# Opening of a fused Mamba-2 scan and hard-swish MLP: C loaded by heads, second weights queued behind the row sums, decode steps reordered

## The chip, the cores and the metric

The kernel runs on one core of one Trainium2 chip. The metric is the device time of one execution in microseconds (us), lower is better. Engines are named as in the profile: PE (TensorE), PEld (its weight loads), DVE (VectorE), ACT (ScalarE), POOL (GpSimd), SP (SyncE, which only issues DMAs here). A "q" behind a name is the engine's sequencer.

## The reference

Two blocks follow each other. The first is a chunked state-space scan over x (4, 8, 768, 32), a (4, 8, 768), B and C (4, 8, 768, 16); the second an MLP of width 2048 on the result, seen as 3072 tokens of 256.

```python
log_a = np.log(np.clip(a, 1e-06, 1.0))
for c in range(nc):                                  # chunks of 32 tokens
    cum = np.cumsum(la, axis=-1)
    L = np.exp(cum[:, :, :, None] - cum[:, :, None, :]) * causal
    CB = np.einsum('bhin,bhjn->bhij', Cc, Bc)
    y_intra = np.einsum('bhij,bhjd->bhid', CB * L, xc)
    y_inter = np.einsum('bhin,bhnd->bhid', Cc, state) * np.exp(cum)[..., None]
    y[:, :, sl] = y_intra + y_inter
    state = decay_full * state + np.sum(Bx, axis=2)  # Bx: B x^T, faded to the chunk's end
...
h = x @ w_in                                         # (3072, 256) @ (256, 2048)
g = h * np.clip(h + 3.0, 0.0, 6.0) / 6.0
out = (g @ w_out).astype(np.float32)                 # (3072, 2048) @ (2048, 256)
```

The weights w_in and w_out arrive as 64-bit floats and everything else as 32-bit.

## The kernel before

The kernel takes the sequence in six chunks of 128 tokens (`NC` = 6), all 4 batches (`NB`) and 8 heads (`NH`) at once. Each chunk goes through the scan and then, as 512 tokens, through the MLP; chunk c + 1's scan is woven into chunk c's MLP. The first chunk has no MLP to hide behind, so the program begins with an **opening** that runs chunk 0's scan alone. The order of all instructions is written out by hand; each engine takes its own in that order, and waits where data or a buffer is not there.

**Decay matrices of chunks 0 and 1.** `a` is loaded, its logarithm taken, and the row sums formed in two parts: `add_up(ends_at[0])` for the first 256 tokens, `add_up(ends_at[1])` for the rest (L269). The first part is split in three bf16 pieces (`in_three`), and TensorE builds the differences of the sums in PSUM: `diff_mask` (L336), `mask_again` (L343), `diff_less` (L348), `diff_pick` (L357). ScalarE takes the exponentials (`diff_exp`, L365; `first_eto`, L376). The second part is stored to DRAM by `store_rows` as `cum_e` and `cum_d` (L286, L288) and read back later, broadcast over rows. `turn_cum` and `by_token` turn the sums of chunks 2 to 5 (L316, L319), for use much later.

**Chunk 0's scan.** `turn_b` transposes B on TensorE (L422) and copies it as `bT` (L431). C comes by another way: `pairs_first` loads it already by pairs of heads in eight DMAs (L101), into a tile whose row is 32 times the pair plus a group of four tokens; `turn_squares` (L465) then turns 32x32 blocks on VectorE, and `part_heads` (L475) makes the two masked copies `cT`. `ends` (L396) and `fade` (L481) run on GpSimd. `scores(0)` multiplies them on TensorE (L530), then forms the chunk's contribution to the state from `xt` (L548). `multiply(0)` takes the part sums out on ScalarE (L564, L574) and applies the decay on VectorE (four L579). `mix(0)` (L625, and L503 for the state) gives y, `keep(0)` copies it out (four L639), `renew(0)` makes the next state (L600, two L558). `busy(n, bank)` issues n matmuls whose result nobody reads (L493). After that `mlp_in` begins (L647): 16 values of f, two matmuls each, in four PSUM banks, with `ramp` (L754, ScalarE) and `times_ramp` (L759, VectorE) behind each; then `first_out` (L772).

**Weights.** w_in and w_out come in four quarters each, i = 0 to 7 (`NP` = 4: i < 4 is w_in, f = 4i to 4i + 3), as raw 64-bit words through three buffers. `load_w(i)` issues the DMA of a quarter (L139), and `decode(i)` turns it into 32-bit floats by bit operations on two engines. A decode is a generator; `weights(i, n)` runs n of its five steps: (1) ACT takes the top words (L198), and with quarter 0 DVE the significand (L201, L205); (2) DVE L215, L217 (and L201 with other quarters); (3) ACT L221 (and L205); (4) ACT L223, and the load of quarter i + 3 when i > 0; (5) DVE L228 and L236, which writes the decoded weights. Quarters 0 and 1 are decoded in the opening, the later ones between the values of f.

**DMA order.** Quarter 0 and B of chunk 0 are issued by ACT, everything else by SP in this order: `a`, eight of C, x, quarter 1, `cum_e`, `cum_d`, quarters 2, 3 and 4, then chunk 1's loads. A DMA's completion is counted in one of eight semaphores; a DMA that reuses a semaphore waits for the one before it there, so the sixth C load waits for quarter 0, the seventh for `a`, the eighth for the first C load. Chunks 2 to 5 load B and C by `pairs_first` too.

Of the kernel before, what the change touches and what calls it, by code (L numbers as in the profile page):

```python
# [8 lines left out]
FP32 = mybir.dt.float32  # L9
# [5 lines left out]
ALU = mybir.AluOpType  # L15
# [6 lines left out]
def kernel(  # L22
# [24 lines left out]
    nc = tc.nc  # L47
    P = 128
    NB, NH, S, D = x.shape
# [18 lines left out]
    ps = ctx.enter_context(tc.tile_pool(name="ps", bufs=1, space=PSUM))  # L68
# [17 lines left out]
    def load_bc(c):  # L86

        sl = slice(c * P, (c + 1) * P)  # L90

        def tokens_first(src, queue=nc.sync, **where):
            t = loads.tile([P, NB * NH, N], FP32, **where)
            queue.dma_start(out=t, in_=src[:, :, sl, :].rearrange("b h s n -> s (b h) n"))
            return t

        def pairs_first(src):
            t = loads.tile([P, 2, NB, 4, N], FP32, name="pairs", tag="bc")
            for b in range(NB):
                for h in range(2):  # L100
                    nc.sync.dma_start(  # L101
                        out=t[:, h, b].rearrange("s a n -> s (a n)"),
                        in_=src[b, h:NH:2, sl, :].rearrange("h (s a) n -> h s (a n)", a=4))
            return t

        if 0 < c < TURN:
            bcs[c] = [tokens_first(C, name="C", tag="bc")]
        Bs[c] = tokens_first(B, nc.scalar if c == 0 else nc.sync, name="B", bufs=1)
        if c == 0:
            bcs[c] = [pairs_first(C), Bs[c]]  # L110
        elif c < TURN:
            bcs[c].append(Bs[c])
        else:
            bcs[c] = [pairs_first(C), pairs_first(B)]

    def load_x(c):
        sl = slice(c * P, (c + 1) * P)
        xts[c] = loads.tile([P, NB * NH, D], FP32, name="xt", bufs=1)
        nc.sync.dma_start(out=xts[c], in_=x[:, :, sl, :].rearrange("b h s d -> s (b h) d"))
# [8 lines left out]
    def load_w(i, queue=nc.sync):  # L128

        raw = loads.tile([P, NK * FP * 2 * P], U32, name="raw", bufs=NRAW)  # L130
        if i < NP:
            cols = slice(2 * i * FP * P, 2 * (i + 1) * FP * P)
            src = moe_w_in[:, cols].rearrange("(k p) f -> p k f", p=P)
            dst = raw.rearrange("p (k f) -> p k f", k=NK)
        else:
            r0 = (i - NP) * FP * P
            src = moe_w_out[r0:r0 + FP * P, :].rearrange("(k p) m -> p k m", p=P)
            dst = raw.rearrange("p (k m) -> p k m", k=FP)
        queue.dma_start(out=dst, in_=src)  # L139
        raws[i] = raw  # L140
# [1 line left out]
    load_w(0, nc.scalar)  # L142
    load_bc(0)
    load_x(0)
    load_w(1)
    nc.scalar.preload_act_table_set("natural_log_exp_and_others")


# [6 lines left out]
    def conceal_in(t, pattern):  # L155
# [24 lines left out]
        out=head, in_=head, pattern=[[-2 * N, NQ], [-N, 2]], compare_op=ALU.is_ge,  # L180
        fill=0.0, base=0, channel_multiplier=1)
    nc.gpsimd.affine_select(
        out=head, in_=head, pattern=[[2 * N, NQ], [N, 2]], compare_op=ALU.is_ge,
# [3 lines left out]
    def decode(i):  # L187

        n = NK * FP * P
        top = raws[i].bitcast(U16).rearrange("p (n w) -> p n w", w=4)[:, :, 3]
        lo, hi = (raws[i].rearrange("p (n w) -> p n w", w=2)[:, :, w] for w in range(2))
        s = att.tile([P, n], U16, name="ws")
        e = att.tile([P, n], U16, name="we")
        m = att.tile([P, n], U32, name="wm")
        nc.scalar.copy(out=s, in_=top)  # L198

        def significand():  # L200
            nc.vector.tensor_scalar(  # L201
                out=m, in0=hi, scalar1=0xFFFFF, scalar2=0x100000,
                op0=ALU.bitwise_and, op1=ALU.bitwise_or)
            yield
            nc.vector.scalar_tensor_tensor(  # L205
                out=m.bitcast(FP32), in0=lo, scalar=2.0 ** -32, in1=m, op0=ALU.mult,
                op1=ALU.add)
            yield

        parts_m = significand()  # L210
        if i == 0:
            next(parts_m)
            next(parts_m)
        yield
        nc.vector.tensor_scalar(  # L215
            out=e, in0=s, scalar1=0x7FF0, scalar2=None, op0=ALU.bitwise_and)
        nc.vector.tensor_scalar(  # L217
            out=s, in0=s, scalar1=0x8000, scalar2=None, op0=ALU.bitwise_and)
        next(parts_m, None)
        yield  # L220
        nc.scalar.activation(e.bitcast(BF16), e, AF.Relu, bias=bias_hi, scale=-8.0)  # L221
        yield
        nc.scalar.activation(e, e.bitcast(BF16), AF.Relu, bias=bias_lo, scale=-1.0)  # L223
        next(parts_m, None)
        if i and i + NRAW < 2 * NP:
            load_w(i + NRAW)
        yield
        nc.vector.tensor_tensor(out=e, in0=e, in1=s, op=ALU.bitwise_or)  # L228
        m, e = m.bitcast(FP32), e.bitcast(BF16)
        if i < NP:  # L230
            dst = w_in[i]
            m, e = (t.rearrange("p (k f) -> p k f", k=NK) for t in (m, e))
        else:
            dst = w_out[:, (i - NP) * FP:(i - NP + 1) * FP, :]
            m, e = (t.rearrange("p (k f) -> p k f", k=FP) for t in (m, e))
        nc.vector.scalar_tensor_tensor(  # L236
            out=dst, in0=m, scalar=2.0 ** -20, in1=e, op0=ALU.mult, op1=ALU.mult)
# [47 lines left out]
    def store_rows():  # L285
        nc.sync.dma_start(  # L286
            out=cum_e[1:].rearrange("c g p -> g c p"), in_=cum_c[:, 1:])
        nc.sync.dma_start(  # L288
            out=cum_d[2:].rearrange("c a g i -> g (c a) i"),
            in_=cum[:, 2 * P:].rearrange("g (k i) -> g k i", i=HT))  # L290
# [21 lines left out]
    cum_n = const.tile([P, NC, G], FP32, name="cum_n")  # L312
# [3 lines left out]
            nc.tensor.transpose(out=c_ps[:, c], in_=cum_c[:, c], identity=ident[:G, :G])  # L316

    def by_token(c_ps):
        nc.vector.tensor_scalar(  # L319
            out=cum_n[:, 2:], in0=c_ps[:, 2:], scalar1=-1.0, scalar2=None, op0=ALU.mult)  # L320


    yTs, states, mids, bTs, bss, tmps = {}, {}, {}, {}, {}, {}
# [17 lines left out]
    def mask_again(c, b):  # L341

        nc.tensor.matmul(  # L343
            out=ds[c, b], lhsT=ident_h, rhs=hide.unsqueeze(1).to_broadcast([P, NH, HT]),
            start=True, stop=True)
# [45 lines left out]
    def ends(c, b):  # L391

        if b == 0:
            bss[c] = att.tile([P, G, N], FP32, name="bs", bufs=1)
        hs = slice(b * NH, b * NH + NH)
        nc.gpsimd.tensor_tensor(  # L396
            out=bss[c][:, hs], in0=Bs[c][:, hs],
            in1=Ls[c][:, b, :, HT - 1:HT].to_broadcast([P, NH, N]), op=ALU.mult)
# [8 lines left out]
    def turned(c):  # L407
        if c not in bTs:
            bTs[c] = [att.tile([P, NB, P], FP32, name="bT", bufs=1),
                      att.tile([P, NB, 2, P], FP32, name="cT", bufs=1),  # L410
                      att.tile([P, NB, P], FP32, name="csT", bufs=1)]
        return bTs[c]

    def turn_ps(c, j):

        if c < 2:
            return ps.tile([P, NB, P], FP32, name="t_ps", tag=f"f{2 * j if c else 1}")
        return ps_o.tile([P, NB, P], FP32, name="t_ps", tag="o")

    def transposes(c, j, t_ps):  # L420
        for b in range(NB):
            nc.tensor.transpose(  # L422
                out=t_ps[:, b],
                in_=bcs[c][j][:, b * NH:(b + 1) * NH].rearrange("s h n -> s (h n)"),
                identity=ident)

    def turn_b(c):

        t_ps = turn_ps(c, 1)
        transposes(c, 1, t_ps)  # L430
        nc.scalar.copy(out=turned(c)[0], in_=t_ps)  # L431
# [58 lines left out]
    def busy(n, bank):  # L490

        for _ in range(n):
            nc.tensor.matmul(  # L493
                out=bank.rearrange("p (b i) -> p b i", b=NB), lhsT=ident,
                rhs=ident.unsqueeze(1).to_broadcast([P, NB, P]), start=True, stop=True)
# [514 lines left out]
    def weights(i, n):  # L1010
        for _ in range(n):
            next(parts[i], None)
# [12 lines left out]
    row_signs()  # L1025
    add_up(ends_at[0])
    in_three()
    for b in range(3):
        mask_again(0, b)
    diff(0, 0, 1)  # L1030
    diff(0, 2, 3)
# [5 lines left out]
    weights(0, 1)  # L1037
    for b in range(NB):
        ends(0, b)
    turn_b(0)  # L1040
    diff(1, 0, 1)
    weights(0, 1)
    diff_exp(1, 2)
    diff_exp(1, 3)
    turn_squares(bcs[0][0], turned(0)[2])
# [1 line left out]
    fade(0, HALF[1], nc.gpsimd)  # L1047
    add_up(ends_at[1])
    store_rows()
    load_w(2)  # L1050
    weights(0, 1)
    busy(2, ps.tile([P, NB * P], FP32, name="d", tag="f3"))
    scores(0)
    multiply(0)
    load_w(3)
    c_ps = ps.tile([P, NC, G], FP32, name="c_ps", tag="f1")
    turn_cum(c_ps)
    busy(1, ps.tile([P, NB * P], FP32, name="d", tag="f0"))
    weights(0, 1)
    weights(1, 1)  # L1060
    by_token(c_ps)
    mix(0)
    keep(0)
    weights(1, 3)
    renew(0)
    weights(1, 1)
    load_eto(1)
    load_bc(1)
    load_x(1)
# [175 lines left out]
```

## Time and profile before

| What | us |
|---|---|
| time, median of 3 runs (339.91 to 340.11) | 339.91 |
| profiled execution, its own time | 339.78 |
| its span in the trace | 337.6 |
| PE busy | 330.6 (98%) |
| DVE busy | 234.5 (69%) |
| ACT busy | 199.4 (59%) |
| POOL busy | 123.9 (37%) |
| first `mlp_in` matmul (L647) begins, in the chain of waits | 22.60 |
| first `first_out` matmul (L772) begins, in the chain of waits | 50.27 |

Times in the trace count from the span's start. A row of the timeline has start, length, engine, line, operation, output and inputs, a count, and in brackets the idle time before it and what ended that. The chain of waits goes back from the last instruction to whatever released each step. DMA rows stand at the time of issue and their length is the issue, not the transfer.

### The profile page before, as it was taken

How to read it: one execution, taken by the hardware profiler on the slowest of the kernel's cores; microseconds unless marked ns; L12 is line 12 of the kernel's file. 1: busy time of each engine (PE TensorE's matmuls, PEld its weight loads, DVE VectorE, ACT ScalarE, POOL GpSimd, SP SyncE). 2: the span in 40 equal slices, each digit the busy share in tenths (PEclk: the TensorE clock that was granted, in tenths of full speed). 3: DMA queues.
4: the chain of work that ended last, by engine and by line, in shares of the span. 5: the costliest groups of instructions: out<-in, count | busy, mean ns of one | idle time of the engine just before them, and what ended most of it. 6: DMA issues, size and time to landing. Idle time of an engine off the chain costs nothing.

```text
span 337.6 us, 8192 instructions
## 1 busy us (share of the span) xinstructions
PE 330.6 (98%) x3337; PEld 265.4 (79%) x3337; DVE 234.5 (69%) x380; ACT 199.4 (59%) x418; POOL 123.9 (37%) x123
## 2 busy tenths in 40 slices
PE   6999999999999999999999999999999999999996
PEld 2554448888888888888888888888888888899995
DVE  6699999998399739755339556355477355599974
ACT  4769878757986670576461576570486030577661
POOL 3300000290184799089813079911079800000000
PEclk9999999999999999999999999999999999999999
DMA  8999968042590215258107267101160001110001
GB/s 174 165 316 201 208 219 184 2 54 76 139 142 1 57 37 139 33 72 78 33 13 156 33 83 69 28 4 17 27 81 2 2 2 18 26 21 2 1 2 62
DMA packets 89605, 25.15 MB, mean 75 GB/s; under 512 B 82208, under 2 KB 85952, under 8 KB 89056
## 3 DMA queue, kind: packets, MB, share of 16 engines
q1 hardware_dynamic: 85184, 23.33, 37.5%
q10 hardware_dynamic: 4384, 1.31, 1.8%
q8 instruction: 26, 0.43, 0.5%
q14 instruction: 11, 0.09, 0.1%
HBM read 21.33 MB, written 3.29 MB: 73 GB/s over the span
## 4 chain that ended last, share of the span: by engine, by line
PE 94%; DMA 3%; DVE 1%; SPq 1%; issue 0%; DVEq 0%
PE h L715 33%; PE wb L914 13%; PE wc L914 8%; PE o L772 8%; PE h L647 8%; PE wa L914 8%; PE o_end L880 6%; PE y L625 3%; PE y L503 2%; PE cb L530 2%; DMA raw<-in_moe_w_in_dram 2%; DMA pairs<-in_C_dram 1%; PE y L548 1%; SPq L101 1%; PE o_end L898 1%; PE sp L548 0%
## 5 line engine op out<-in xcount | busy, mean ns | idle before, releaser
L759 DVE SCALAR_TENSOR_TENSOR gT<-gT,h 128x512 f32<-128x512 f32 x96 | 64.8, 684 | 33.8 <-ACT gT L754 32.2
L754 ACT ACTIVATE gT<-h,half 128x512 f32<-128x512 f32 x96 | 65.2, 685 | 25.6 <-PE h L715 23.6
L735 ACT ACTIVATE h<-h 128x512 f32<-128x512 f32 x66 | 38.2, 585 | 39.0 <-PE h L715 38.8
L715 PE MATMUL h<-y_hi,w_part 128*128 128x512 f32 x160 | 51.5, 407 | 0.0
L715 PE MATMUL h<-y_less,w_part 128*128 128x512 f32 x160 | 50.1, 399 | 0.0
L715 PE MATMUL h<-y_lo,w_part 128*128 128x512 f32 x160 | 49.5, 395 | 0.0
L818 POOL TENSOR_TENSOR s<-gT 128x512 f32<-128x512 f32 x16 | 23.8, 1490 | 46.7 <-DVE gT L759 46.7
L715 PEld LDWEIGHTS h<-y_lo,w_part 128*128 128x128 f32 x160 | 30.0, 188 | 7.3
L715 PEld LDWEIGHTS h<-y_hi,w_part 128*128 128x128 f32 x160 | 30.0, 188 | 6.8 <-DVE gT L759 0.2
L715 PEld LDWEIGHTS h<-y_less,w_part 128*128 128x128 f32 x160 | 29.2, 188 | 6.0 <-ACT h L735 0.2
L385 ACT ACTIVATE L<-L,cum_n 128x64 f32<-128x64 f32 x128 | 31.6, 336 | 0.0
L772 PE MATMUL o<-w_out,gT 128*128 128x256 f32 x128 | 28.8, 381 | 0.0
L647 PE MATMUL h<-yT,w_in 128*128 128x512 f32 x64 | 27.7, 594 | 0.0
L772 PEld LDWEIGHTS o<-w_out,gT 128*128 128x128 f32 x128 | 24.1, 190 | 3.8 <-issue 0.5
L647 PEld LDWEIGHTS h<-yT,w_in 128*128 128x128 f32 x64 | 12.1, 190 | 14.9 <-issue 13.2
L158 POOL TENSOR_SCALAR_AFFINE_SELECT L<-L 64x1024 f32<-64x1024 f32 (+1 forms) x16 | 20.4, 1281 | 8.5 <-DMA L<-cum_d 8.0
L579 DVE TENSOR_TENSOR L<-L,cb 128x512 f32<-128x512 f32 x24 | 15.0, 681 | 11.7 <-PE cb L530 11.7
L403 POOL TENSOR_TENSOR tmp<-state,eto 128x256 f32<-128x256 f32 x5 | 3.2, 643 | 52.8 <-ACT eto L389 48.9
L818 POOL TENSOR_TENSOR s<-gT,s 128x512 f32<-128x512 f32 x16 | 21.7, 1364 | 0.9
L396 POOL TENSOR_TENSOR bs<-B,L 128x128 f32<-128x128 f32 x24 | 11.2, 486 | 29.5 <-ACT L L385 20.9
L880 PE MATMUL o_end<-v_pair,g_pair 128*128 128x256 f32 x120 | 21.1, 281 | 0.0
L818 POOL TENSOR_TENSOR gT<-gT 128x512 f32<-128x512 f32 x16 | 20.4, 1279 | 0.9
(140 smaller groups left out, 593.0 us busy)
## 6 DMA issues: line engine op xcount, KB each, us to landing
raw<-in_moe_w_out_dram SPq DMA_DIRECT2D x4, 1024.0 KB
L<-cum_d SPq DMA_DIRECT2D x8, 512.0 KB
xt<-in_x_dram SPq DMA_DIRECT2D x6, 512.0 KB
raw<-in_moe_w_in_dram SPq DMA_DIRECT2D x3, 1024.0 KB
out_dram<-back SPq DMA_DIRECT2D x128, 16.0 KB
pairs<-in_C_dram SPq DMA_DIRECT2D x40, 32.0 KB
eto<-cum_e SPq DMA_DIRECT2D x20, 64.0 KB
B<-in_B_dram SPq DMA_DIRECT2D x5, 256.0 KB
```

Source lines behind the costliest of these rows:

```text
L158: nc.gpsimd.affine_select(out=t[rows], in_=t[rows], pattern=pattern, compare_op=ALU.is_ge, fill=-1e5, base=base, channel_multiplier=-1)
L385: nc.scalar.activation(Ls[c][:, b, h], Ls[c][:, b, h], AF.Exp, bias=cum_n[:, c, g:g + 1])
L579: nc.vector.tensor_tensor(out=Ls[c][:, :, hs], in0=Ls[c][:, :, hs], in1=cbs[c][q], op=ALU.mult)
L647: nc.tensor.matmul(out=h, lhsT=w_in[f // FP][:, j, f % FP * P:(f % FP + 1) * P], rhs=yTs[k][:, j].rearrange("p b i -> p (b i)"), start=(j ...
L715: nc.tensor.matmul(out=hs_[k, f], lhsT=w[j][:, f % FP * P:(f % FP + 1) * P], rhs=y[:, j], start=(start and j == 0), stop=True, skip_group_ ...
L735: nc.scalar.activation(h, h, AF.Copy, scale=1.0 / EPS + 1.0)
L754: nc.scalar.activation(gTs[k][:, f], h, AF.Relu, bias=half, scale=1.0 / 6.0)
L759: nc.vector.scalar_tensor_tensor(out=g, in0=g, scalar=1.0, in1=h, op0=ALU.min, op1=ALU.mult)
L772: nc.tensor.matmul(out=o[:, b % 2], lhsT=gTs[0][:, f, b * P:(b + 1) * P], rhs=w_out[:, f], start=(f == 0 and b % 2 == 0), stop=True, skip_ ...
L818: nc.gpsimd.tensor_tensor(out=o, in0=p_, in1=q_, op=op)
L880: nc.tensor.matmul(out=ends_["cross" if n == 2 else "squares"][b], lhsT=g_parts[t][n][:, b * P:(b + 1) * P], rhs=w, start=(t == 0 and b < ...
L914: nc.tensor.matmul(out=bank[:, slot], lhsT=lhs[:, j], rhs=rhs[:, j], start=(clear and j == 0), stop=True, skip_group_check=True)
```

## The change

Line numbers here and below are those of the kernel before. Six things change:

1. `pairs_first` still makes eight DMAs, but one for each head with all batches, instead of one for each batch and half of the heads. The destination of one is 32 rows by 4 batches by 64 elements, the source the same, with the 32 groups of four tokens outermost; before, it was 128 rows by 64 elements, with four heads outermost in the source. The pieces have 64 elements in both.
2. `load_w(1)` moves from behind `load_x(0)` to behind `store_rows()`: on SP it now follows `cum_e` and `cum_d`.
3. In `decode`, quarter 1 runs its significand operations (L201, L205) in steps 1 and 2 instead of 2 and 3; quarter 0 and the later ones are unchanged.
4. `by_token` is a ScalarE multiplication instead of a VectorE one, and stands ahead of quarter 0's last step, the mix and `keep`.
5. `mask_again` also runs for batch 3; quarter 0's third step (L221) moves ahead of `turn_b(0)`; `busy(2, ...)` ahead of `scores(0)` is gone, `busy(1, ...)` stays.
6. All five steps of quarter 1 follow `renew(0)`; before, L198 stood ahead of `keep`, L215 to L223 ahead of `renew`, the fifth step behind it.

```diff
         def pairs_first(src):
             t = loads.tile([P, 2, NB, 4, N], FP32, name="pairs", tag="bc")
-            for b in range(NB):
-                for h in range(2):
-                    nc.sync.dma_start(
-                        out=t[:, h, b].rearrange("s a n -> s (a n)"),
-                        in_=src[b, h:NH:2, sl, :].rearrange("h (s a) n -> h s (a n)", a=4))
+            for h in range(NH):
+                rows = slice(h // 2 * 32, h // 2 * 32 + 32)
+                nc.sync.dma_start(
+                    out=t[rows, h % 2].rearrange("s b a n -> s b (a n)"),
+                    in_=src[:, h, sl, :].rearrange("b (s a) n -> s b (a n)", a=4))
             return t
...
     load_x(0)
-    load_w(1)
...
         parts_m = significand()
-        if i == 0:
-            next(parts_m)
+        for _ in range(2 - i):
             next(parts_m)
...
     def by_token(c_ps):
-        nc.vector.tensor_scalar(
-            out=cum_n[:, 2:], in0=c_ps[:, 2:], scalar1=-1.0, scalar2=None, op0=ALU.mult)
+        nc.scalar.mul(cum_n[:, 2:], c_ps[:, 2:], -1.0)
...
-    for b in range(3):
+    for b in range(NB):
         mask_again(0, b)
...
     for b in range(NB):
         ends(0, b)
+    weights(0, 1)
     turn_b(0)
     diff(1, 0, 1)
-    weights(0, 1)
...
     store_rows()
+    load_w(1)
     load_w(2)
     weights(0, 1)
-    busy(2, ps.tile([P, NB * P], FP32, name="d", tag="f3"))
     scores(0)
     multiply(0)
     load_w(3)
     c_ps = ps.tile([P, NC, G], FP32, name="c_ps", tag="f1")
     turn_cum(c_ps)
     busy(1, ps.tile([P, NB * P], FP32, name="d", tag="f0"))
+    by_token(c_ps)
     weights(0, 1)
-    weights(1, 1)
-    by_token(c_ps)
     mix(0)
     keep(0)
-    weights(1, 3)
     renew(0)
-    weights(1, 1)
+    weights(1, 5)
     load_eto(1)
```

## The prediction

> **What bounds the kernel now.** I read the page first, its chain of work that ended last.
> ```profile
> PE 94%; DMA 3%; DVE 1%; SPq 1%; issue 0%; DVEq 0%
> ```
> TensorE sets the end almost everywhere; 6% do not belong to it, and the next view, the chain in order of time for the first 60 us, shows that they lie in the opening.
> ```profile
> 0.80 5.94 DMA raw<-in_moe_w_in_dram
> ...
> 8.91 4.00 DMA pairs<-in_C_dram
> ...
> 13.09 1.17 DVE csT L465
> ...
> 14.28 0.89 DVE cT L475 x2
> ...
> 15.30 1.25 PE cb L530 x59
> ...
> 17.90 0.43 PE c_ps L316 x4
> ...
> 22.60 27.66 PE h L647 x64
> 50.27 9.93 PE o L772 x46
> ```
> Columns: start, length, work. Until 13 us the chain is the first weights and then C's eight loads; after that it goes C's turn, scores, mix, and from 22.60 the first linear layer. Third, the timeline by engine, for what is moved.
> ```profile
> 10.65 0.39 ACT L376 ACTIVATE eto<-e_ps 128x256 f32<-128x256 f32 x1
> 11.95 0.59 ACT L431 COPY bT<-t_ps 128x512 f32<-128x512 f32 x1 [0.90 <-PE t_ps L422]
> 18.75 1.15 ACT L198 COPY ws<-raw 128x1024 uint16<-128x1024 uint16 x1 [0.53 <-DMA raw<-in_moe_w_in_dram]
> 22.65 0.37 ACT L639 COPY yT<-y 128x256 f32<-128x256 f32 x1 [0.26 <-PE y L503]
> 22.92 1.15 ACT L221 ACTIVATE we<-we,bias_hi 128x1024 bf16<-128x1024 uint16 x1
> 26.01 1.23 DVE L236 SCALAR_TENSOR_TENSOR w_in<-wm,we 128x1024 f32<-128x1024 f32 x1
> 33.62 1.22 DVE L236 SCALAR_TENSOR_TENSOR w_in<-wm,we 128x1024 f32<-128x1024 f32 x1
> 41.11 1.22 DVE L236 SCALAR_TENSOR_TENSOR w_in<-wm,we 128x1024 f32<-128x1024 f32 x1
> 48.12 1.23 DVE L236 SCALAR_TENSOR_TENSOR w_out<-wm,we 128x1024 f32<-128x1024 f32 x1
> ```
> The first four rows show ScalarE idle for 0.90 us before bT and busy with the decode of the second weights around `keep`. The L236 rows end the decodes of quarters 1 to 4, at 27.24, 34.84, 42.33, 49.35: 7.6, 7.5 and 7.0 us apart, while TensorE takes 27.66/16 x 4 = 6.9 us for the four f that use a quarter. Quarter 4 (w_out's first) is done 0.92 us before its first use at 50.27. The decode is a second bound right behind TensorE.
>
> **C's loads.** In the trace's completion events each C load raises its semaphore by one lump and four single steps; loads that lead with 128 rows (B, xt, raw) or 32 rows (pre, cum_e) do it in sixteen. So a load that leads with 4 heads runs on 4 of the 16 queues, and B agrees: twelve of its parts land by 9.28, four at 10.18 to 11.15. With 32 rows outermost each C load should run on sixteen, with 64 of its 256-byte pieces in each instead of 256 in four. Issue: the sixth load still waits for the first weights (6.74) and starts at 6.76; the seventh took 1.49 us against full queues, now 0.57 like the sixth; the eighth starts at about 8.0 instead of 8.91. C loads of later chunks land 2.5 to 3.1 us after their issue. That gives 10.5; bounds 9.8 (pieces hidden) and 12.9 (as before).
>
> **To the scores.** VectorE has been free since 10.23. L465 starts at 10.5 + 0.18 = 10.7, the two L475 end 2.08 later at 12.8, add_up (L269) 3.19 later at 13.9. ScalarE now does L221 (1.15) ahead of bT: 11.06 to 12.2, mostly in the idle 0.90; bT ends at 12.8 instead of 12.54, a loss only if it comes last; behind it stand two L365 and L223, not wanted before 16 us. TensorE ends chunk 1's differences at 12.96 as now (B's transposes begin at 11.28, and TensorE was not free before 11.17, so an earlier B brings nothing). All three meet: scores at 13.0 instead of 15.30, **2.3 us earlier**. `busy(2)` (1.98) would hold TensorE until 14.9, so its removal is needed for 1.9 of these; alone it would bring nothing, since 0.43 us of idle follows it. The fourth `mask_again` costs 0.43, under TensorE's idle 0.52 before 7.50.
>
> **Scores to the linear layer**, 15.30 to 22.60, keeps its links and its 7.3 us: add_up is done (13.9) before the products L579 start (14.3), and VectorE's second L579 holds c_ps as now. xt is issued at 8.6 instead of 9.59; its four late parts took 2.7 us after C, the others about 4, so it lands at 13.2 to 14.5; L548 wants it at 14.1, and until 14.7 a delay hides behind L579. GpSimd's fade (L481, 1.51) follows L475 and ends at 14.3, wanted only in the mix. `by_token` on ScalarE costs between 0.21 (L257) and 0.39 (L376) where ScalarE waits for the mix, with the copies of `keep` behind it; on VectorE it was 0.28 behind L236, and ended at 21.10, in the mix. I take 0 for it, bounds -0.1 and 0. The layer starts at 20.3.
>
> **The second weights.** Their load leaves its place behind xt (10.43) for one behind cum_e and cum_d, which wait for add_up: cum_e 13.9, and by the old spacing (16.31 to 17.17) the load 0.86 later, 14.8. The first weights took 5.94 from issue to landing, the last quarter 5.6 with the queues empty: 20.4 to 20.7, where it landed at 18.73 before. Queued behind it are quarters 2 and 3, needed at 25 and 31 us; they follow 3 to 4 us apart and are in time. L198 of quarter 1 now stands behind `keep`, whose last copy ends at 23.02 - 2.3 = 20.7. So the load arrives as it is wanted, with nothing to spare: 0, bounds 0 and +2.4 (below).
>
> **Decode of quarter 1.** L198 20.7 to 21.9, L215 21.9 to 22.35, L221 at 22.4, against 22.92. VectorE finishes quarter 0 (L228, L236) at 18.6 and `renew` (L600, 2 x L558: 1.03) at 19.7, takes L201 when the load lands, and waits for L198: `renew` ahead of the decode is free, and the early L201 too (0.7 in a wait). From L221 on the steps are as before, so the chain of decodes moves by **0.55 us** only, and L236 ends at 26.7. VectorE sets its pace: 4 x 0.68 (L759) and 0.42 + 0.43 + 0.69 + 1.22 + 0.69 + 1.22 for a quarter make 7.4, less some overlap.
>
> **Sum.** TensorE would come to w_out at 50.27 - 2.3 = 47.97; quarter 4 is ready at 49.35 - 0.55 = 48.80 and TensorE starts 0.13 later (as 15.17 to 15.30): 48.93. The gain is 50.27 - 48.93 = **1.34**; 0.96 of 2.3 is given back as waits in the first layer. Behind it the next slacks are larger: w_out's second quarter has 1.45 (55.75 for 57.2), chunk 1's L579 ends 1.4 before the mix at 77.98, and the later C and B loads are on no wait of the chain. The profiled execution took 339.78 (span 337.6, 2.2 around it), the median is 0.13 higher: 339.91 - 1.34 = 338.6.
>
> **Rivals.** (a) The second weights come late. From 20.7 on each us costs one, since decodes have no other cover; from 22.0 the gain is gone. One load (issue 39.94) had fifteen parts by 45.54 and one at 47.47, 7.5 after issue; its own row before is 8.3, behind xt. That gives 22.3 to 23.1, 1.6 to 2.4 late: 340.2 to 341.0. For it: a single slow queue appears in three of eight weight loads; against it: the queues are empty at 14.8. This is the way to slower. (b) C's loads land no sooner, at 12.9: scores at 15.3, L198 behind `keep` at 23.0 and L221 at 24.65, 1.73 later than now; less the 0.8 of slack at w_out, +0.9: 340.8. The break-even is a landing at about 12. The Trainium skill (DMA: Bandwidth & Descriptors, "Rules for kernel authors") speaks for it: transfers split over disjoint partitions share the same engines and only serialize. The trace does not bear this out, as the loads before did not use all sixteen. (c) Decode keeps up at its fastest pace, 7.0 a quarter: all 2.3 stay, 337.6. Against it: two of three steps are 7.5. (d) TensorE slows without `busy`. Its first eleven 512-column matmuls come 0.43 apart (8 in 3.57 us), from 7.50 the spacing is about 0.22, after 5.4 us of work. Were that lost before the linear layer, 5.4 us would do the work of 2.7 and w_out be reached at 50.7: +0.4, 340.3. Against it: before, small matmuls fill 14.9 to 22.5 but for one `busy(1)`, which stays, and the layer starts at 0.43 a pass; the longest gap that I expect is 0.5 us. The Trainium skill (TensorE: Matmul & The Clock Gate, "What's actually happening") has the gate close only after some 3.4 us idle; by that rule nothing changes here.
>
> **Chances.** Forecast 0.62, (a) 0.14, (b) 0.06, (c) 0.10, (d) 0.05, others 0.03. Within 0.2% means 0.68 us, about what measuring this kernel can tell from no change. Half of (a) and most of (d) stay within it, and in a few of the forecast's cases the load is 0.7 late. Faster 0.70, same 0.14, slower 0.16. The range goes from (c), 337.6, to the middle of (a), 340.6.
>
> **To be seen after.** Sixteen steps for each C load, L465 at 10.4 to 11, scores at about 13.0, the first L647 at 20.3, quarter 1's L198 at 20.7 behind `keep` and not behind DMA, L236 ends near 26.7, 34.2, 41.8 and 48.8, short waits of L647 on VectorE (about 1 us together), the first L772 at 48.9. Wrong if L465 waits for C beyond 12, if L198 waits for the load, or if L647's first pass takes over 0.43.

## The result: slower, and the profile after

| | median of 13 runs, us | range |
|---|---|---|
| before | 340.23 | 339.64 to 342.23 |
| after | 342.82 | 339.56 to 345.77 |

The ratio is 1.0053, 95% interval 1.003 to 1.0077: the kernel became slower by half a per cent, some 1.8 us. The medians take all runs; the ratios here and below leave out those more than 1.5% above the fastest of their kernel, which are three of after here and five of the twelve of "after, with `busy(2)` back" below, its profiled one among them. The forecast of 338.6 and its range are wrong.

The profiled execution of after is the quickest of its thirteen, 339.56 us with a span of 337.4, and the only one with a granted clock of 1.00 throughout (the share of TensorE's full clock that the profile records); the other twelve show means of 0.984 to 0.998. So the profile shows what the change does when almost nothing disturbs it, and a second question is what happens in the others. Line numbers of after are two or three lower (L644 is the old L647, L219 the old L221, L234 the old L236). The chain of waits by engine:

```profile
PE 85%; DVE 6%; DMA 4%; ACT 3%; issue 1%; SPq 0%
```

TensorE had 94% of it before. The same chain in order of time (start, length, work; in this view a DMA's length runs from its issue to its landing):

```profile
1.73 6.55 DMA pairs<-in_C_dram
...
8.29 7.03 DMA xt<-in_x_dram
...
18.95 0.28 issue
...
21.96 1.04 ACT ws L197
...
23.48 1.16 ACT we L219
...
41.67 1.24 DVE w_in L234
...
42.95 7.13 PE h L644 x16
50.09 12.07 PE o L769 x55
```

x has taken C's place as the last load that TensorE waits for, and from 21.96 the chain runs through the decode of the second weights until w_in's last quarter is written at 42.91. `first_out` begins at 50.09 instead of 50.27: in this run the change is worth 0.18 us up to there. The timeline shows where the forecast 2.3 us went (in brackets the idle time before, and what ended it):

```profile
11.82 1.11 DVE L462 STREAM_TRANSPOSE csT<-pairs 128x512 f32<-128x512 f32 x1 [1.85 <-DMA pairs<-in_C_dram]
14.00 1.20 PE L527 MATMUL cb<-cT,bT 32*64 32x128 f32 x64 [1.44 <-DVE cT L472]
15.46 1.16 PE L545 MATMUL y<-xt,bs 64*32 64x64 f32 x64 [0.27 <-DMA xt<-in_x_dram]
23.48 1.15 ACT L219 ACTIVATE we<-we,bias_hi 128x1024 bf16<-128x1024 uint16 x1 [0.49 <-DVE we L213]
```

C landed at 11.64, not 10.5, so the scores start at 14.00 and not at 13.0, and TensorE, without `busy(2)`, stands idle for 1.44 us. One row of the chain above is new: 0.28 us of "issue" in the middle of the mix, a time in which TensorE waits for nothing that the profile knows. It turned out to be the key.

### The profile page after: what moved, and what is told of

It reads as the page before. It is cut to its first block, busy times and chain, and to the rows that moved or that the text cites. A ratio compares the mean times of both kernels' runs of the same rounds, so it can differ in the third digit from the quotient of the medians.

```text
span 337.4 us, 8188 instructions
## 1 busy us (share of the span) xinstructions
PE 328.6 (97%) x3334; PEld 264.0 (78%) x3334; DVE 235.1 (70%) x379; ACT 198.6 (59%) x419; POOL 124.7 (37%) x123
## 4 chain that ended last, share of the span: by engine, by line
PE 85%; DVE 6%; DMA 4%; ACT 3%; issue 1%; SPq 0%
PE h L712 30%; PE wb L911 13%; PE o L769 8%; PE wc L911 8%; PE wa L911 8%; PE o_end L877 6%; PE y L622 3%; PE y L500 2%; PE h L644 2%; DMA xt<-in_x_dram 2%; DVE gT L756 2%; DMA pairs<-in_C_dram 2%; PE cb L527 2%; PE y L545 1%; ACT we L219 1%; DVE w_in L234 1%
## 5 line engine op out<-in xcount | busy, mean ns | idle before, releaser
L644 PE MATMUL h<-yT,w_in 128*128 128x512 f32 x64 | 28.2, 599 | 0.4 <-DVE w_in L234 0.4
L644 PEld LDWEIGHTS h<-yT,w_in 128*128 128x128 f32 x64 | 11.8, 190 | 16.0 <-issue 12.2
L393 POOL TENSOR_TENSOR bs<-B,L 128x128 f32<-128x128 f32 x24 | 11.9, 519 | 28.0 <-ACT L L382 19.6
```

The costliest lines, as they stand in the source:

```text
L644: nc.tensor.matmul(out=h, lhsT=w_in[f // FP][:, j, f % FP * P:(f % FP + 1) * P], rhs=yTs[k][:, j].rearrange("p b i -> p (b i)"), start=(j ...
```

## The experiments

Four kernels of a group ran on one chip, with the kernel before among them. Times are medians. In the first group theory A says that TensorE's clock drops because fillers are missing in the opening, B that it drops because the first layer waits for weights, C that the result is an accident.

**The same kernel again.** No edit.

> The changed kernel itself, once more. Its runs so far went from 339.56 at a mean granted TensorE clock of 1.0 to 345.8 at 0.984. Theory A (the clock gate closes for some windows because filler matmuls are missing in the opening): clock below 1 in most runs, times 340 to 345 beside 340 of the kernel before, and if the profiled run is one of these, the clock row of its page is below 9 within the first 60 us. Theory B (the gate closes because the first linear layer waits for decoded weights): the same times, the low clock after 27 us. Theory C (an accident of that occasion, not of the kernel): as the kernel before, within 0.7 us, clock 1.0.

343.45 us (341.84 to 345.37), ratio 1.0091 [1.0062, 1.012]; clock 0.985 to 0.995 in every run. So it is no accident (theory C falls). Its profiled run took 341.84, 2.3 more than that of after. Two idle stretches have grown, 0.76 us in the products for the state and 1.13 us in the mix, both put down to "issue". The view by stretches (from:to, length, busy time of PE, PEld, DVE, ACT, POOL with counts, granted clock, DMA share, GB/s), cut at the moments when the clock changes, shows the consequence:

```profile
12.68:16.09 3.41, 1.53 (x77) 1.15 (x72) 3.10 (x6) 1.83 (x3) 1.50 (x1) 1.00 0.37 46
16.09:19.51 3.42, 3.42 (x68) 1.88 (x68) 3.38 (x6) 1.06 (x4) 0.00 (x0) 0.50 0.85 221
```

TensorE was busy for 1.53 us of 3.41, and had half its clock for the next 3.41, in which it was busy all the time.

**After, with `busy(2)` back.**

```diff
     weights(0, 1)
+    busy(2, ps.tile([P, NB * P], FP32, name="d", tag="f3"))
     scores(0)
```

> The changed kernel with the two filler matmuls ahead of the scores put back. They take 1.98 us; TensorE is free at 12.55, so they end at 14.5, and the scores start at 14.5 instead of 14.0. Theory A: clock 1.0 in every run, 339.6 to 340.4. Theory B: the waits of the first layer stay or grow, clock still below 1, 341 to 344. Theory C: 340 as all others.

344.18 us (339.39 to 346.05), ratio 1.0056 [1.0026, 1.0087]. A alone falls: the wait ahead of the scores is filled, yet nine of twelve runs are below a clock of 1.00. The timeline of the profiled run (346.05) has the reason:

```profile
18.73 0.91 PE L622 MATMUL y<-L,xt 64*32 64x64 f32 x56
22.99 0.44 PE L622 MATMUL y<-L,xt 64*32 64x64 f32 x8 [3.36 <-issue]
```

TensorE stops for 3.36 us in the middle of the mix, with its inputs there, ahead of the first layer (so not B either), and the clock is halved from 21.96 to 32.20.

**Before, without `busy(2)`.**

```diff
-    busy(2, ps.tile([P, NB * P], FP32, name="d", tag="f3"))
     scores(0)
```

> The kernel before without the two filler matmuls ahead of the scores; nothing else. In the trace of before they end 0.43 us ahead of the scores, so no wait moves. Theory A: clock below 1 in most runs, times spread from 340 to 345. Theory B: clock 1.0, 339.9 (no wait in the first layer). Theory C: 339.9.

341.23 us, ratio 1.0026 [1.0002, 1.0051]. The filler does matter: with 2.14 us of idle ahead of the scores and PE busy for 1.46 of 3.42 us, the profiled run had half the clock for 6.83 us.

**Before, with only the new C loads.** The edit is the `pairs_first` hunk of the change.

> The kernel before with the new form of C's loads alone. C should land near 11.6 instead of 12.9, the turn start near 11.8 and the masked copies end near 13.9; the fillers end at about 14.5 to 14.9, so the scores start there instead of 15.30: 0.4 to 0.8 earlier, and the decode of quarter 1, behind keep as before, moves by as much. Theory A and B: clock 1.0, 339.1 to 339.6. If the second weights or x land later for it, the gain is smaller: 339.9.

345.30 us, ratio 1.0139 [1.0112, 1.0165], where 339.1 to 339.9 was expected: worse than the whole change, with all of before's fillers in place. Here too TensorE stops in the mix, for 2.38 us of "issue".

**What the stops have in common.** I counted TensorE's records in the trace, weight loads and matmuls together, in order of time. In the runs so far, every stop of over 0.1 us put down to "issue" begins at record 450 or 706, to within one, whatever is computed there; the two are 256 apart. And the page (of after, and of all others alike) has a DMA queue of its own for instructions:

```profile
q8 instruction: 26, 0.43, 0.5%
```

These 26 packets have 16,384 bytes each, which is 64 bytes for each of 256 records. Counted from 0, the last packet to end before TensorE goes on is number k where the stop is at record 450 + 256k: in all 22 stops of the profiled runs, those of the experiments below included (the latest at record 6081, with packet 22). No stop comes ahead of record 450. I read this as TensorE's program arriving in blocks, by the same DMA engines that carry the loads. Theory D: a block's packet that is asked for while loads are queued waits behind them, and TensorE stops at the block's first instruction. The trace's DMA records, with TensorE's idle at the block's first instruction (us; the last five rows are experiments below):

```
                       x       packet of     2nd weights  packet of    idle at   half
                       issued  block 450     issued       block 706    450/706   clock
before                 9.6     10.7 - 11.8   10.4, 17.2   17.8 - 18.8  0/0       0
after                  8.3     12.5 - 14.0   15.8         16.9 - 18.4  0/0.28    0
after again            8.1     13.4 - 14.9   15.7         19.4 - 20.3  0.76/1.13 3.41
after, busy(2)         8.1     13.4 - 14.9   15.8         20.6 - 21.6  0.25/3.36 10.24
before, no busy(2)     9.8     11.1 - 12.3   10.5, 17.3   18.6 - 19.5  0/0       6.83
before, new C loads    8.2     13.5 - 15.0   8.7, 16.0    21.3 - 22.3  0/2.38    6.83
after, weights held    7.9     13.7 - 15.0   16.9         17.4 - 18.7  0.74/0    6.83
first load early       8.2     13.6 - 15.1   8.7, 17.6    17.8 - 18.7  0.52/0.14 0
and decode early       8.1     13.7 - 15.2   8.7, 17.5    18.3 - 19.2  0.70/0.42 0
and x held             9.4     10.4 - 11.5   9.8, 17.4    18.4 - 19.3  0/1.14    3.41
after, old C loads     9.6     10.8 - 11.9   17.1         17.3 - 18.3  0/0       6.83
```

In 17 of the 18 such stops in the openings of all profiled runs TensorE goes on 1.20 to 1.46 us after its packet has ended (0.86 in the other). The Trainium skill (Runtime: NRT & Kernel Launch, "Instruction fetch mechanics") describes just such blocks of 16 KiB or 256 instructions, fetched by the engine's own DMA queue, and has their cost mostly hidden; the size agrees with the trace, the hiding does not. The next four kernels test D against C': it is the C loads' traffic, and where the blocks begin has nothing to do with it.

**Before, with more TensorE instructions.** Nothing else is changed: no load, no wait, no buffer.

```diff
+        ds[c, b] = d
+        if c == 0 and b < 3:
+            for _ in range(59 if b == 0 else 0):        # 19 in the other kernel
+                nc.tensor.matmul(
+                    out=d[:HT, 0, :16], lhsT=ident_h[:, :HT], rhs=hide[:, :16],
+                    start=True, stop=True)
+            return
         nc.tensor.matmul(
             out=d, lhsT=ident_h, rhs=hide.unsqueeze(1).to_broadcast([P, NH, HT]),
             start=True, stop=True)
-        ds[c, b] = d
```

> Before, with three of the first masking products left out (they are written again later) and 59 narrow products (64 x 16) in their place: 112 more TensorE instructions ahead of everything else, no load, wait or buffer changed. Theory D (TensorE's program arrives in blocks of 256 instructions, one 16,384-byte packet of queue q8 each; a block that is asked for after the second weights' loads are issued arrives some 4 us later, and TensorE stands still at the block's first instruction): the blocks now begin 112 instructions earlier in the work, one is asked for at about 18.8 us, behind the loads issued at 17.2, its packet runs at about 21.6 and TensorE stands still for 1.5 to 2.8 us in the second half of the products with x and L, ahead of the first layer. 342 to 345 us, and a granted clock of 0.99 or below in most runs. Theory C' (it is the C loads and their traffic, not where the blocks begin): as before, 339.9 to 340.7, clock 1.0.

> The same with 19 narrow products: 32 more TensorE instructions. Theory D: the blocks are asked for ahead of the second weights' loads or needed only in the first layer, so no stall over 0.5 us: 339.8 to 340.8, clock 1.0 in most runs. If the missing masking products alone disturb the clock (theory A): as slow as the 59.

With 59: 358.65 us, ratio 1.0524 [1.049, 1.0558]. With 19: 340.46, ratio 0.9993 [0.9975, 1.0011]. Where the blocks begin is worth 18 us; of the theories here only D has any stop there. D had foretold the stop at record 962 (2.82 us measured), but not one of 0.94 us at record 706, nor that it goes on, so that its 342 to 345 us were far too low. The 19 are as fast as D says, but their profiled run has a stop of 0.63 us at record 706, over the 0.5 that D allowed. PE's waits of the 59 have

```profile
PE y L509 <- issue: 6.6, 4, 2.2
PE y L631 <- issue: 3.8, 2, 2.8
```

(us in total, times, the longest). The four at L509 lie in the scans of later chunks, at records 3010, 4033, 5057 and 6081, all 194 past a multiple of 256 to within one; before has none of them. Stops account for 10.4 of the 18 us; half a clock in three windows of 3.41 us and a later start make up part of the rest, which I did not take apart further.

**After, with the second weights held back** behind the second multiplication of L with the scores, by a one-element copy into their tile.

```diff
+        if behind is not None:
+            nc.gpsimd.tensor_copy(raw[:1, :1].bitcast(FP32), behind)
         queue.dma_start(out=dst, in_=src)
...
-    load_w(1)
-    load_w(2)
...
     multiply(0)
+    load_w(1, behind=Ls[0][:1, 0, 2, :1])
+    load_w(2)
     load_w(3)
```

> After, with the three loads of second weights held back until the second of the four multiplications of L with the scores has ended (a one-element copy by GpSimd into the first load's tile): issue at about 17.2 instead of 15.8. Theory D: TensorE's block is asked for at 15.5 to 16.1, ahead of them, its packet starts before 17.5, no stall over 0.5 us at the products with x and L; clock 1.0 in most runs; the first of these weights is decoded 1.3 us later, which the first layer waits for: 340.5 to 341.5. Theory C': the C loads are as they were, so 342 to 344 as after, or more for the later weights.

340.27 us, ratio 1.0008 [0.9986, 1.0031], just below what D expected: by the ratios against before, loading the weights 1.1 us later saves 1.5 us (after, 1.0053) to 2.8 us (after again, 1.0091). The request is as late as in "after again" (record 450 runs at 16.2 and 16.1), but the packet starts at 17.4 instead of 19.4 and the stop in the mix is gone. Ten of twelve runs have a clock of 0.999 or 1.00. The stop at 450 remains; in the profiled run (341.45) it and 1.25 us ahead of the scores still halved the clock.

**The first of these loads early again** (behind x, as before), the other two held, and `busy(2)` back.

```diff
     load_x(0)
+    load_w(1)
...
+    busy(2, ps.tile([P, NB * P], FP32, name="d", tag="f3"))
     scores(0)
     multiply(0)
+    load_w(2, behind=Ls[0][:1, 0, 2, :1])
     load_w(3)
```

> After, with the first of these loads back behind x's load (8.7 us), the second and third held back as above, and busy(2) back ahead of the scores. Theory D and the clock's windows together: TensorE has no idle stretch over 0.7 us ahead of the first layer, clock 1.0 in most runs, and the weights are in time: 338.8 to 339.8, faster than before. Theory C': 342 to 344.

339.97 us, ratio 0.9984 [0.9968, 1.0001], clock 0.998 to 1.00 in every run. The median lies just above the expected range; 0.66 us of stops are left at the two blocks.

**The same, with one step of the decode back ahead of the mix.**

```diff
     by_token(c_ps)
     weights(0, 1)
+    weights(1, 1)
     mix(0)
     keep(0)
     renew(0)
-    weights(1, 5)
+    weights(1, 4)
```

> The kernel with the first load early, with one step of these weights' decoding (ACT's copy) back ahead of the stage's results, as before has it. Theory D (blocks of TensorE's program): the stalls stay those of the kernel with the first load early (0.5 us at the block in the scores, 0.1 us at the next); the chain of the decoded weights is 1 to 1.5 us earlier and TensorE's wait of 0.36 us for w_in at 43.4 us is gone: 339.3 to 339.9, 0.2 to 0.4 below the kernel with the first load early. If the weights were not what the layer waited for: no change from that kernel.

339.28 us (338.56 to 339.71), ratio 0.9969 [0.9957, 0.9981]: **0.3% faster than before**, which after is not. The kernel with the first load early ran on another chip; by the two ratios the step is worth some 0.5 us, with intervals that overlap a little. In the profiled run (339.28), TensorE's only waits from the first scores until the first layer has ended are two blocks of its own program; the chain in order of time has

```profile
15.91 0.70 issue
...
20.02 0.42 issue
...
22.77 27.66 PE h L647 x64
50.43 4.75 PE o L772 x22
```

and the wait for w_in (0.36 us in after and in the kernel above) is gone. But `first_out` begins at 50.43 here, no earlier than in the profile of before (50.27), so not all of the gain is explained. Some 0.4 us of it lies outside the trace's span: time less span is 1.8 us in the four kernels that hold a load back, the one above and "weights held" included, and 2.2 in all others. Why, and where within the span the rest arises (median span 337.5, beside 338.2 of before on the same chip), is not shown.

**And x's load held until the first exponential of L.**

```diff
-    load_x(0)
-    load_w(1)
...
+    diff_exp(0, 0)
+    load_x(0, behind=Ls[0][:1, 0, 0, :1])
+    load_w(1)
-    for b in range(NB):
+    for b in range(1, NB):
         diff_exp(0, b)
```

> The same, with x's load (and the first second-weights load behind it) held back until the first of the exponentials for L has ended: issue at about 9.4 instead of 8.2, as in before (9.6). Theory D: the block that starts in the scores is asked for ahead of x's 4096 pieces again, its packet starts at 10.7 to 12.0 instead of 13.4 to 13.7, and the stall of 0.5 to 0.8 us in the scores or the state's products is gone; x lands at 14.8 to 15.6, just in time: 338.9 to 339.8. Rival: that packet is late because of C's pieces on all queues, not x's: it starts at 13 or later all the same, and x's later landing costs up to 0.5 us more: 339.8 to 340.5.

341.57 us, ratio 1.0037 [1.0012, 1.0062]. The mechanism came out as D says, the time did not: block 450's packet starts at 10.4 and its stop is gone, so x's load, or the weights right behind it, was what delayed it; in after, where no weights follow x, that packet is late too (12.5). But the weights behind x were issued 1.1 us later too, record 450 runs 1.1 us earlier, and block 706's packet now meets those weights: a stop of 1.14 us in the mix. One was cured and the other made worse.

**After, without the opening's B** (GpSimd writes 0.5 into its tile, so B is left out of chunk 0).

```diff
+        if c == 0:
+            Bs[c] = loads.tile([P, NB * NH, N], FP32, name="B", bufs=1)
+            nc.gpsimd.memset(Bs[c], 0.5)
```

> After, without the opening's load of B (GpSimd writes 0.5 into its tile): 4096 of the opening's pieces are gone. If C's landing at 11.6 is set by the pieces that all 16 queues share (theory P): C's loads land 0.3 to 0.5 us behind each other from about 4 us on, the last at 10.0 to 10.6, and the sixth issue waits less than at 3.5 to 6.8. If the end of the last load lies 4.0 us behind its issue whatever else is on the queues (theory Q): the last lands at 4.0 behind its issue, 11.3 to 11.7 if that is still 7.6.

In the one run of this kernel C's last load lands at 9.15 instead of 11.64, 1.8 us behind its issue instead of 4.0, though the last two loads are issued about as late as ever (6.99 and 7.34). Q falls. P has the direction right: without B's 4096 pieces of 64 bytes, which all 16 queues share with C, C lands 2.5 us sooner. The course is not P's, though: no C load lands before 7.3 us (4 expected), all eight then land within 1.9, ahead of P's range, and the sixth is issued at 3.95 instead of 6.80, which this run does not separate from B's pieces. The turn of C starts early (10.51 us in the timeline), and the kernel takes 343.57 us all the same, with stops of 0.93 and 3.36 us at the two blocks: in this run the earlier C bought nothing, with the blocks late.

**After, with C's loads as before.**

> After, with C's loads as they were before (4 heads outermost). Theory D: xt is issued at 9.6 again and the block that starts in the scores has its packet at 10.7 to 11.1; the second weights are issued at about 17, behind the request of the next block (16.2), so that the packet starts before 18.5 and there is no stall over 0.7 us at the products with x and L; the gap ahead of the scores (2.1 us, no busy(2)) closes the clock in some runs; the weights come 1.1 us later than in after and the first layer waits for them: 340.8 to 342.3, below after's 343. If the other parts of the change (weights issued later, decoded later) are what makes after slow: 342.5 or more.

342.42 us, ratio 1.0066 [1.0048, 1.0083], between the two expectations. Both packets are in time and no block stops TensorE, as D says. What is left is the missing filler (2.17 us idle ahead of the scores, and half the clock for the next 6.83) and the late weights (0.36 us of wait for w_in). So the C loads are not the only part of the change that costs something.

## Why the prediction was wrong, point by point

The forecast was 1.34 us less, and some 1.8 more were measured. Two steps failed. In the sum, C's landing was sized 1.1 us too early, which takes nearly all of the 1.34. And the sum has no term for the instruction blocks, and put idle time's price in clock at nothing: in "after again" the stops were 0.76 and 1.13 us, the clock was halved for 3.41, and the run took 341.84 us.

- **C's loads.** That each load would run on sixteen queues was right: the trace has sixteen completion steps for each instead of five. (The 64 pieces in each queue are those of all eight loads together; one load has 8.) The landing was the mis-sized term: 10.5 was taken from later chunks, where nothing else is loaded, and it was 11.64. Sixteen queues also means sixteen shared with B; in the kernel without B the landing was 9.15. The eighth issue came at 7.63 (8.0 forecast).
- **To the scores.** The steps from C on were right in length, the start 1.0 late: 14.00. The expectation that the longest gap is 0.5 us failed with it: TensorE was free at 12.55 and idle for 1.44, just where the filler had been taken out.
- **x** was issued at 8.29, before the 8.6 forecast; fifteen of its parts landed by 14.21, the last at 15.32, 0.27 late for TensorE. The step that failed is to cost an earlier load by its own landing alone: its pieces stood in front of TensorE's next block.
- **The second weights** landed 5.58 us behind their issue, at 21.43, before ScalarE was free from `keep` (21.86): rival (a) did not happen. But no step asked what else is queued behind these loads; block 706 was.
- **The decode chain** was right as a chain. It starts 1.16 late: 1.0 with the scores, the rest behind them, where 0.27 for x and 0.28 for the block were partly made up. So L219 comes at 23.48 against 22.4 forecast and 22.92 before, and the four decodes end 0.56 later than before, not 0.55 earlier. The sum of 1.34 less some 1.1 gives 0.2, and 50.27 - 50.09 = 0.18 was measured. That is the run whose clock held: 339.56 us, beside 339.78 in the profiled run of before, no change to speak of.
- **Rival (d), the clock, at 0.05,** named the place of the loss but not its cause and had its price too small (340.3). The Trainium skill (TensorE: Matmul & The Clock Gate, "What's actually happening") let the gate close only after some 3.4 us idle, and I took from it that nothing changes. The runs contradict that: in the openings the clock fell (but for one case, below) behind windows with PE busy for 0.59 to 1.53 us of 3.41, with no idle stretch over 1.12 us in "after again". Window length and the two levels agree with the page.
- **What nothing in the prediction had:** TensorE's own program as a transfer that competes with the loads. Before, x (9.6) and the later second weights (17.2) are issued late enough for both packets; the change moved each of them 1.3 us forward. This is shown by holding each of the two back (in either kernel the stop of that load's own block goes) and by shifting the blocks alone (18 us).

It remains open why block 706's packet starts only 1.2 us after record 450 in the profiled run of after, 3.3 in "after again" and 4.4 in "after, busy(2)"; the table fits a race between a request at about 16 us and the weights' issue at 15.8. Open too is what ends a half-clock period: a window with PE busy throughout ended it in "after again" but not in "after, busy(2)", where it lasted three windows. And "and x held" lost its clock behind a window with 2.48 us busy, while the clock held behind one with 1.60 us at the end of after, so busy time by the records does not decide it alone. How much of a kernel's loss is the stops and how much the clock was not taken apart. The fourth `mask_again`, the earlier L221 and `by_token` on ScalarE were not run alone; no wait of TensorE in the profile of after is put down to them.

## What to carry to other kernels

Moving a load forward moves it in front of what the DMA engines carry later, and in this kernel that included TensorE's own instructions. Where TensorE waits for "issue" at places 256 instructions apart, look at when the 16,384-byte instruction packets ran and which load was issued just ahead of them; hold that load back, or shift the blocks, before anything else. And take a filler out only after the wait that it covers has been seen to be gone.

## What the runs showed of the hardware that was not expected

- TensorE's program comes in 16,384-byte packets, each for 256 records by the spacing of the stops, taking 0.9 to 2.2 us on queue q8 in these traces, and behind the second weights they start up to 4.4 us after TensorE enters the block before. In 17 of the 18 stops in the openings TensorE goes on 1.20 to 1.46 us after the packet's end.
- 59 small TensorE products in place of three wide ones (112 instructions more), ahead of an otherwise unchanged program, cost 18 us; 19 in their place (32 more) cost nothing measurable.
- In the openings the granted clock halved for one to three windows of 3.41 us behind a window in which TensorE was busy for 0.59 to 1.53 us (2.48 in one case), though no idle stretch was over 3.36 us, and in "after again" the longest in that window was 1.12. It held behind 1.98 us in the opening of after, and later in the kernel with 59 it fell behind 1.25 and 1.83: these runs give no sharp limit.
- Eight loads of 256-byte pieces that share all queues with 4096 pieces of 64 bytes landed 2.5 us later than in the one run without those.
